# Dense weights converted in PSUM banks, and a new order of products and background work, in a fused attention, expert and dense kernel

## The chip, the cores and the metric

The kernel runs on one core of a Trainium2 chip. The metric is the device time of one execution in microseconds (us). The core's engines each work through their own queue in order: PE (TensorE, matrix products; PEld are its weight loads), DVE (VectorE), ACT (ScalarE), POOL (GpSimd) and SP (SyncE, which only issues DMAs here). They meet through semaphores.

## What is computed

The reference chains three layers. Attention through 32 memory slots per head gives 4608 rows of 512. Each row is then sent to one of 8 experts (at most 576 rows each, handed out greedily by the score), whose layer is two products with a ReLU between. The result goes through one dense layer with a hard-swish:

```python
def _moe_ref(x, w_gate, w1, w2):
    ...
    for idx in order:                       # all (token, expert) scores, largest first
        tok, e = (int(idx) // E, int(idx) % E)
        if assigned[tok] >= 0 or counts[e] >= cap:
            continue
        assigned[tok] = e
        counts[e] += 1
    ...
    for e in range(E):
        mask = assigned == e
        h = np.maximum(x[mask] @ w1[e], 0.0)
        out[mask] = h @ w2[e]

def _moe2_ref(x, w_in, w_out):              # w_in 512 x 2048, w_out 2048 x 512
    h = x @ w_in
    relu6 = np.clip(h + 3.0, 0.0, 6.0)
    g = h * relu6 / 6.0
    return g @ w_out
```

Inputs of the dense layer are 64-bit floating-point weights, which the kernel reads as pairs of 32-bit integers and converts on the chip.

## The kernel before

All products after attention are made from pairs of 16-bit numbers (a high and a low part), three matmuls for one product. The program falls into these stages:

- Attention, up to about 255 us.
- For each expert k, `l1(k)` (first layer, 192 matmuls of 288 columns, PSUM tiles named `p` with `xt` as input) and `l2(k)` (second layer, tiles `p` with `h` as input). The expert's weights (`w`) are fetched into `wst`, scaled and split by `weights()`: ACT writes the high part, DVE (for four pieces of T = 3, POOL) the low part.
- `unit(k)`: the dense layer on 512 rows. Its output `h @ w_in` is made with seven block products per step instead of eight (a Strassen-Winograd scheme). One unit has eight steps (`step(i)`); a step runs seven products of six matmuls of 256 columns into three PSUM tiles `pq`, `pr`, `pw`, with `take` (ACT) and `join` (DVE, L568 `h<-pw,h` and so on) moving the sums out, then `gate`: ACT, DVE (`h<-h,h`, 128x512), ACT and POOL work out the hard-swish. After each product but some, `pend` adds one deferred piece of the second dense product (six matmuls of 512 columns into `acc`).
- The order is l1(0) l2(0) l1(1) l2(1) unit 0 unit 1 l1(2) l2(2) l1(3) l2(3) unit 2 l1(4) l2(4) unit 3 and so on, and units 6, 7, 8 at the end.

Beside this chain of products run background jobs, as Python generators at build time: `routes()` (who goes to which expert: eight rounds per expert, each with matmuls `rtp` and short DVE instructions, and at the end one-hot matrices `OH`), `gathers()` (rows `xg` fetched by index, transposed by PE into `xp`, written to `xt`), `weights()`, `ysplit(k)` (scales the expert's output `y` and splits it into seven tiles `st`, ACT then DVE), and the dense weights. A build-time clock (`CK.now`, with a cost per instruction for DVE, ACT and POOL in `V_`, `A_`, `G_`) decides where a job's next instruction is put; `yield t` asks to go on at time t, `yield t, V_` only once DVE's queue is worked off by that clock as well. On the chip none of these times exist: only the order in each queue stays. `R_OK[0]` is the highest expert whose routing may begin.

The dense weights: 32 loads `dst` (128x1024 integers each). `dense_piece` makes 512 floats from each with four DVE instructions of 512 elements (one TENSOR_SCALAR, three SCALAR_TENSOR_TENSOR) on `cva`, an SBUF tile, and two or three of ACT. The w_out pieces are then split by ACT and POOL into `wo`; two w_in pieces together go through `wino_weights`, where POOL and ACT make the seven blocks, write them to DRAM (`wid`), and `stream` fetches them again for each step as `ws`.

PSUM: seven banks in a ring (`bank`), of which stages before unit 0 use the first four; from unit 0 on all seven are in use: four for `acc`, three for `pq`, `pr`, `pw`, with `xp` and `amx` in between. Every instruction of the background jobs stands under L568, every matmul under L619, transposes under L624, since helpers record them.

Of the kernel before, what the change touches and what calls it, by code (L numbers as in the profile page):

```python
# [20 lines left out]
def attn_moe_kernel(ctx: ExitStack, tc: tile.TileContext, q, k, v, phi, w_gate, w1, w2, w_in, w_out, out):  # L21
# [560 lines left out]
    A_ = Eng(nc.scalar, 0.06, 0.00097)  # L582
# [50 lines left out]
    def bank_free():  # L633
        return any(BANK[i][0] for i in RING if i < NB[0])

    def bank(done):
        if not bank_free():
            b, CK.busy = CK.busy, False
            need(bank_free)
            CK.busy = b  # L640
        i = next(i for i in RING if i < NB[0] and BANK[i][0])
        RING.remove(i)
        RING.append(i)
        BANK[i] = done
        return f"bk{i}"

    def mm_tile(shape, name, done):
        return ps.tile(shape, F32, name=name, tag=bank(done), bufs=1)
# [355 lines left out]
    def weights():  # L1004
        for T in range(2 * E):
            k, which = divmod(T, 2)
            while k not in EIX or T == 3 and 1 not in XI:
                yield CK.now + 0.3
# [26 lines left out]
            for n in range(9):  # L1035
# [14 lines left out]
                if n and n - 1 in PS.get(T, ()):  # L1050
# [4 lines left out]
                    yield CK.now + 0.1, A_  # L1055
                    WC[T] = c + i, tl
                elif n:
                    yield rd[n - 1], V_
                    c, i = divmod(n - 1, 2)
                    cs = slice(i * 512, i * 512 + 512)  # L1060
                    V_.scalar_tensor_tensor(tl[c][:, 1, cs], WST[T, c][0][:, cs], s[:, 0:1], tl[c][:, 0, cs],
                                            op0=OP.mult, op1=OP.subtract)
                    if i and T + 1 < 2 * E and T != 2:
                        spawn(w_later(T + 1, c))
                    yield CK.now + 0.1, A_
                    WC[T] = c + i, tl
# [11 lines left out]
    def gathers():  # L1078
        for k in range(E):
# [7 lines left out]
            def fetch(i):  # L1087
# [5 lines left out]
                elif k == 1 and i > 1:  # L1093
                    if i % 2 == 0:
                        big.append(wk.tile([128, 2, 512], F32, name="xg", tag=f"wst{i // 2 - 1}"))
                    xg = big[-1][:, i % 2]
# [124 lines left out]
    WA, WX, NWS, CUR = {}, {}, [0], [0]  # L1221
# [9 lines left out]

    def dense_piece(which, j, done, st, ready):
        yield ready, V_
        L, Hw = st[:, 0::2], st[:, 1::2]
        while not spare(0):
# [4 lines left out]
        V_.tensor_scalar(a, Hw, 3, 0x3FFFFFF8, op0=OP.logical_shift_left, op1=OP.bitwise_and)  # L1240
        yield V_.t - 0.3, V_
        V_.scalar_tensor_tensor(a, Hw, -(1 << 30), a, op0=OP.bitwise_and, op1=OP.bitwise_or)
        yield V_.t, V_
        s2 = Hw.bitcast(F32)
        A_.activation(s2, s2, AF.Square)
        V_.scalar_tensor_tensor(a, L, 29, a, op0=OP.logical_shift_right, op1=OP.bitwise_or)
        yield max(V_.t, A_.t) + HOP, V_
# [172 lines left out]
    def ysplit(k):  # L1420
# [49 lines left out]
        for i, src, r in ((A11, t1, 0.0), (A12, u1, 0.0), (A22, u2, 0.0), (S1Y, x1, r1), (S2Y, x2, r2), (S3Y, t2, r3),  # L1470
# [85 lines left out]
    def unit(k):  # L1556
# [5 lines left out]
        def step(i):  # L1562
# [4 lines left out]
            if k == 0 and i == 6:  # L1567
                R_OK[0] = 3
# [78 lines left out]
            spawn(join("q", 3, False), first=True)  # L1647
            pend(2)
# [59 lines left out]
```

## Time and profile before

| | us |
|---|---|
| median of 3 runs (lowest to highest) | 1551.49 (1549.43 to 1551.62) |
| the profiled execution | 1555.25 |
| its span on the core | 1553.5 |
| PE busy in the span | 1362.9 |
| DVE / ACT / POOL busy | 984.9 / 811.2 / 602.1 |
| the chain that ended last: PE / DVE | 64% / 18% |

The profiled execution lies 3.76 us over the median; 1.75 us of it are outside the span. An engine's busy time says how much it works, not whether it is waited for: that is read in a stretch of the program at a time, from the waits of PE, which has the most work by far.

### The profile page before, as it was taken

To read this page: it belongs to the slowest core of one execution; us is meant where nothing else is said; L and a number is where in the kernel's file an instruction comes from. 1 tells how busy PE (TensorE), PEld (TensorE's weight loads), DVE (VectorE), ACT (ScalarE), POOL (GpSimd) and SP (SyncE) were. 2 spreads that over 40 slices of the span, in tenths; PEclk is the share of its full clock that TensorE was granted. 3 is DMA by queue.
4 is the path that set the end of the run, shared out by engine and by line. 5 is a ranking of instruction groups with operands and counts; after the bars stand their busy time and mean duration, and the time that the engine had idled before them with its cause. 6 is when DMAs were issued, how large, how long until landed. Compare 5 with 4: busy or idle time off the path is not lost.

```text
span 1553.5 us, 27582 instructions
## 1 busy us (share of the span) xinstructions
PE 1362.9 (88%) x10892; PEld 1011.2 (65%) x10892; DVE 984.9 (63%) x2195; ACT 811.2 (52%) x1572; POOL 602.1 (39%) x611
## 2 busy tenths in 40 slices
PE   4788885986558997989899989999999999999998
PEld 4667664764425665869667856875686687666664
DVE  4678877989996676787846584666555423335222
ACT  4667655567655453552664266236646532545443
POOL 5765304366766343230432053135233221334322
PEclk9989996997768998989999999999999999999999
DMA  9865677464632344330342143124232220233331
GB/s 300 288 240 165 196 228 256 148 222 154 197 127 94 109 163 133 106 92 1 132 153 76 55 136 122 52 82 154 98 125 96 96 75 28 95 109 136 109 109 51
DMA packets 82337, 206.27 MB, mean 133 GB/s; under 512 B 10912, under 2 KB 41632, under 8 KB 82208
## 3 DMA queue, kind: packets, MB, share of 16 engines
q1 hardware_dynamic: 66224, 149.98, 28.5%
q0 software_dynamic: 15168, 52.96, 10.3%
q8 instruction: 85, 1.39, 0.4%
q10 hardware_dynamic: 816, 1.57, 0.3%
q14 instruction: 44, 0.36, 0.1%
HBM read 177.23 MB, written 27.26 MB: 132 GB/s over the span
## 4 chain that ended last, share of the span: by engine, by line
PE 64%; DVE 18%; issue 5%; ACT 5%; DMA 3%; POOL 3%; SPq 0%; ACTq 0%; DVEq 0%; POOLq 0%
PE acc L619 21%; PE p L619 18%; PE pq L619 11%; PE pr L619 5%; DVE cva L568 4%; PE pw L619 3%; DVE h L568 2%; PE xa L420 2%; DMA wst<-in_moe_w_dram,ei 2%; DVE w L568 1%; PE kvp L191 1%; ACT h L568 1%; DVE OH L568 1%; DMA kvt<-in_v_dram 1%; ACT wscr L568 1%
## 5 line engine op out<-in xcount | busy, mean ns | idle before, releaser
L619 PE MATMUL acc<-wo,h 128*128 128x512 f16 x1728 | 432.3, 384 | 35.0 <-ACT h L568 33.4
L619 PEld LDWEIGHTS <-ws 128*128 128x128 f16 x3024 | 301.1, 100 | 145.9 <-issue 52.7
L619 PEld LDWEIGHTS <-w 128*128 128x128 f16 x3072 | 336.6, 122 | 71.4 <-DVE w L568 7.6
L568 POOL TENSOR_TENSOR h<-h,h 128x512 f16<-128x512 f32 x144 | 175.2, 1218 | 436.4 <-ACT h L568 434.6
L619 PEld LDWEIGHTS <-h 128*128 128x128 f16 x1728 | 168.5, 99 | 178.6 <-ACT h L568 34.0
L619 PE MATMUL p<-xt,w 128*128 128x288 f16 x1536 | 210.5, 293 | 5.4 <-DVE h L568 2.1
L619 PE MATMUL p<-h,w 128*128 128x288 f16 x1536 | 201.3, 290 | 12.0 <-POOL w L568 4.8
L568 DVE SCALAR_TENSOR_TENSOR h<-h,h 128x512 f32<-128x512 f32 x144 | 111.8, 777 | 85.2 <-ACT h L568 85.2
L568 ACT ACTIVATE h<-pq 128x256 f32<-128x256 f32 x216 | 81.8, 379 | 151.4 <-PE pq L619 148.5
L568 ACT ACTIVATE h<-h,half_c,inv 128x512 f32<-128x512 f32 x144 | 116.8, 811 | 71.6 <-DVE h L568 47.5
L568 POOL DMA_INDIRECT wst<-in_moe_w_dram,ei x64 | 64.7, 1011 | 214.7 <-DVE ei L568 104.9
L568 ACT ACTIVATE h<-h 128x512 f16<-128x512 f32 x144 | 90.0, 625 | 76.7 <-DVE h L568 74.9
L568 ACT ACTIVATE h<-p 128x288 f16<-128x288 f32 x128 | 52.0, 411 | 130.1 <-PE p L619 127.4
L568 DVE SCALAR_TENSOR_TENSOR w<-wst,s,w 128x512 f16<-128x512 f32 x124 | 106.1, 863 | 1.0 <-ACT w L568 1.0
L568 DVE SCALAR_TENSOR_TENSOR cva<-dst,cva 128x512 int32<-128x512 int32 (+1 forms) x96 | 95.2, 1017 | 0.5
L568 ACT ACTIVATE w<-wst,s 128x512 f16<-128x512 f32 x124 | 86.0, 711 | 7.2 <-DVE s L568 4.3
L568 DVE SCALAR_TENSOR_TENSOR h<-p,h 128x288 f16<-128x288 f32 x128 | 57.2, 453 | 47.5 <-ACT h L568 42.6
L568 DVE TENSOR_TENSOR h<-pr,h 128x256 f32<-128x256 f32 x72 | 30.4, 422 | 80.4 <-PE pr L619 76.3
L568 ACT ACTIVATE y<-p 128x288 f32<-128x288 f32 x64 | 26.0, 406 | 104.1 <-PE p L619 101.4
L568 ACT ACTIVATE wscr<-wst 128x1024 bf16<-128x1024 f32 x64 | 67.5, 1054 | 19.1 <-DMA wst<-in_moe_w_dram,ei 18.5
L568 DVE TENSOR_TENSOR h<-pq,h 128x256 f32<-128x256 f32 x72 | 30.3, 421 | 53.8 <-PE pq L619 53.8
L568 DVE TENSOR_TENSOR h<-pw,h 128x256 f32<-128x256 f32 x72 | 30.3, 421 | 53.6 <-PE pw L619 51.2
(548 smaller groups left out, 2332.8 us busy)
## 6 DMA issues: line engine op xcount, KB each, us to landing
ws<-wid SPq DMA_DIRECT2D x72, 896.0 KB
dst<-in_moe_w_out_dram SPq DMA_DIRECT2D x26, 512.0 KB
qt<-in_q_dram SPq DMA_DIRECT2D x8, 1024.0 KB
dq<-in_moe_w_in_dram SPq DMA_DIRECT2D x16, 512.0 KB
xd<-xs SPq DMA_DIRECT2D x32, 256.0 KB
kvt<-in_k_dram SPq DMA_DIRECT2D x7, 1152.0 KB
kvt<-in_v_dram SPq DMA_DIRECT2D x7, 1152.0 KB
dst<-in_moe_w_in_dram SPq DMA_DIRECT2D x15, 512.0 KB
```

The lines of the kernel that those rows point to most:

```text
L191: nc.tensor.matmul(p[i * 64:(i + 1) * 64, g, 0:128], A[:, hp, r, :], KV[b][:, :, hp, r * 64:(r + 1) * 64], start=(r == 0), stop=(r == R - 1))
L420: nc.tensor.matmul(p[r, g], AT[u][:, half, g, r], VB[b][:, g], start=True, stop=True)
L568: r = f(*a, **kw)
L619: nc.tensor.matmul(o, l, r, start=start, stop=stop, skip_group_check=more)
```

## The change

It converts the dense weights in PSUM tiles `cv` of the upper three banks (4 to 6) instead of in SBUF tiles `cva`; the copy to `cva` is made by ACT while it scales. A common turn (`turn`) puts conversion instructions at least 1.15 us apart on the build-time clock. Routing starts at other places, `ysplit` and `weights` wait for ACT and DVE by the clock for k > 1, the fetch of expert 1's second weights no longer waits for its rows (these are gathered into a `ws` buffer instead of `wst`), ACT is taken to cost more by the clock, and from a unit's second step on the products come in another order.

```diff
-    A_ = Eng(nc.scalar, 0.06, 0.00097)
+    A_ = Eng(nc.scalar, 0.08, 0.0011)
...
-    def bank_free():
-        return any(BANK[i][0] for i in RING if i < NB[0])
+    def bank_free(lo=0):
+        return any(BANK[i][0] for i in RING if lo <= i < (7 if lo else NB[0]))
...
@@ weights
-            while k not in EIX or T == 3 and 1 not in XI:
+            while k not in EIX:
...
-                    yield rd[n - 1], V_
+                    yield (rd[n - 1], V_) if k > 1 else rd[n - 1]
...
-                    if i and T + 1 < 2 * E and T != 2:
+                    if i and T + 1 < 2 * E:
                         spawn(w_later(T + 1, c))
...
@@ gathers
                 elif k == 1 and i > 1:
-                    if i % 2 == 0:
-                        big.append(wk.tile([128, 2, 512], F32, name="xg", tag=f"wst{i // 2 - 1}"))
-                    xg = big[-1][:, i % 2]
+                    if i == 2:
+                        big.append(wk.tile([128, 1792], F32, name="xg", tag="ws", bufs=2))
+                    xg = big[-1][:, 512 * i - 1024:512 * i - 512]
...
+    TURN = [0.0]
+
+    def turn():
+        while CK.now < TURN[0]:
+            yield TURN[0]
+        TURN[0] = CK.now + 1.15
+
     def dense_piece(which, j, done, st, ready):
         yield ready, V_
         L, Hw = st[:, 0::2], st[:, 1::2]
+        while not bank_free(4):
+            yield CK.now + 0.1
+        free = [False]
+        pf = mm_tile([128, 512], "cv", free, 4)
+        a = pf.bitcast(I32)
+        yield from turn()
+        V_.tensor_scalar(a, Hw, 3, 0x3FFFFFF8, op0=OP.logical_shift_left, op1=OP.bitwise_and)
+        yield from turn()
+        V_.scalar_tensor_tensor(a, Hw, -(1 << 30), a, op0=OP.bitwise_and, op1=OP.bitwise_or)
+        yield V_.t, V_
+        s2 = Hw.bitcast(F32)
+        A_.activation(s2, s2, AF.Square)
+        yield from turn()
+        V_.scalar_tensor_tensor(a, L, 29, a, op0=OP.logical_shift_right, op1=OP.bitwise_or)
+        yield max(V_.t, A_.t) + HOP
+        yield from turn()
+        V_.scalar_tensor_tensor(pf, s2, GUARD, pf, op0=OP.is_ge, op1=OP.mult)
+        yield V_.t
+        BUSY.remove(done)
         while not spare(0):
             yield CK.now + 0.1
         tag = spare(0)
         BUSY.add(tag)
         a = wk.tile([128, 512], I32, name="cva", tag=tag)
-        V_.tensor_scalar(a, Hw, 3, 0x3FFFFFF8, op0=OP.logical_shift_left, op1=OP.bitwise_and)
...
-        A_.activation(af, af, AF.Copy, scale=SD[which][:, 0:1])
+        A_.activation(af, pf, AF.Copy, scale=SD[which][:, 0:1])
+        free[0] = True
...
@@ wino_weights
-        while 2 * i not in WA:
+        while 2 * i not in WA or len(WG) > len(WX):
...
@@ l1
-        if k > 2:
-            R_OK[0] = k + 1
+        if k == 2:
+            R_OK[0] = 4
...
@@ ysplit
-            yield r
+            yield (max(r, CK.now + 2.0), A_) if k > 1 else r
             A_.activation(ST[k][i][:, 0], src, AF.Copy, scale=s)
-            yield A_.t + HOP
+            yield (A_.t + HOP, V_) if k > 1 else A_.t + HOP
...
@@ step
-            if k == 0 and i == 6:
-                R_OK[0] = 3
+            if i == 4 and k < 2:
+                R_OK[0] = k + 2
+            elif i == 2 and k > 1:
+                R_OK[0] = k + 3
...
             spawn(take("r", 3), first=True)
-            prod("w", 2, True)
-            spawn(join("w", 0, True), first=True)
             pend(2)
+            if not i:
+                prod("w", 2, True)
+                spawn(join("w", 0, True), first=True)
             need(lambda: 0 in st)
             prod("q", 6, False)
             spawn(take("q", 1), first=True)
-            need(lambda: 3 in st)
-            prod("r", 3, False)
-            spawn(join("r", 1, True), first=True)
+            if i:
+                prod("w", 2, True)
+                spawn(join("w", 0, True), first=True)
+            else:
+                need(lambda: 3 in st)
+                prod("r", 3, False)
+                spawn(join("r", 1, True), first=True)
             pend(2)
-            need(lambda: 1 in st)
+            need(lambda: 1 in st and 3 in st)
             prod("q", 7, False)
             spawn(join("q", 3, False), first=True)
+            if i:
+                prod("r", 3, False)
+                spawn(join("r", 1, True), first=True)
             pend(2)
...
```

DVE's queue in unit 0, before: from step 1's join of `pw` to the second `h<-h,h` of step 0's gate. `st` belongs to ysplit(1), `cva` to the conversion.

```order
L568 TENSOR_TENSOR h_5426<-pw,h_5426 128x256
L568 SCALAR_TENSOR_TENSOR cva<-dst,cva 128x512
L568 SCALAR_TENSOR_TENSOR st__5466<-y_4994,sy_5371,st__5466 128x512
L568 SCALAR_TENSOR_TENSOR cva<-dst,cva 128x512 x2
L568 SCALAR_TENSOR_TENSOR st__5467<-y_5160,sy_5371,st__5467 128x512
L568 SCALAR_TENSOR_TENSOR cva<-dst,cva 128x512 x3
L568 SCALAR_TENSOR_TENSOR st__5468<-y_5160,sy_5371,st__5468 128x512
L568 SCALAR_TENSOR_TENSOR cva<-dst,cva 128x512
L568 SCALAR_TENSOR_TENSOR h_5403<-h_5403,h_5324 128x512
L568 SCALAR_TENSOR_TENSOR cva<-dst,cva 128x512
L568 SCALAR_TENSOR_TENSOR st__5469<-sx__5473,sy_5371,st__5469 128x512
L568 SCALAR_TENSOR_TENSOR h_5403<-h_5403,h_5324 128x512
```

The same queue after the change, from step 0's joins of `pr` and `pq` to the second half of its gate (`h_5395`); `cv` is the conversion.

```order
L568 TENSOR_TENSOR h_5321<-pr,h_5321 128x256
L568 SCALAR_TENSOR_TENSOR cv<-dst,cv 128x512
L568 TENSOR_TENSOR h_5321<-pq,h_5321 128x256
L568 SCALAR_TENSOR_TENSOR cv<-dst,cv 128x512
L568 SCALAR_TENSOR_TENSOR h_5395<-h_5395,h_5321 128x512
L568 SCALAR_TENSOR_TENSOR cv<-dst,cv 128x512
L568 TENSOR_REDUCE sy_1f<-amx 128x1
L568 TENSOR_SCALAR sy_5372<-sy_1f 128x1 x2
L568 TENSOR_SCALAR cv<-dst 128x512
L568 TENSOR_SCALAR inv_5448<-sx,s_1_4382 128x1
L568 TENSOR_SCALAR inv_5448<-inv_5448,s_1_4810 128x1
L568 SCALAR_TENSOR_TENSOR h_5395<-h_5395,h_5321 128x512
```

The gate's first half has moved ahead of the `st` of ysplit(1), right behind the joins that it needs.

PE's queue after the change, where l1(3) has ended: the last round of routing expert 4, up to its first one-hot matmul. Six more rows of `rtp<-RH,OH` and six of a second `OH` follow, then the first matmul of l2(3).

```order
L819 LDWEIGHTS S_2708
L819 MATMUL rtp<-CR,S_2708 128x8
L828 LDWEIGHTS onesb
L828 MATMUL rtp<-FL,onesb 128x8
L870 LDWEIGHTS onesb
L870 MATMUL rtp<-ce,onesb 128x8
L897 LDWEIGHTS tri
L897 MATMUL rtp<-tot,tri 128x2
L898 LDWEIGHTS triu
L898 MATMUL rtp<-tot,triu 128x1
L968 LDWEIGHTS OH
L968 MATMUL rtp<-RH,OH 128x10
```

Before, the same routing lies in l2(3); its `ce` matmul stands between products of that layer:

```order
L619 LDWEIGHTS w_3_8410
L619 MATMUL p_8922<-h_8669,w_3_8410 128x288
L870 LDWEIGHTS onesb
L870 MATMUL rtp<-ce,onesb 128x8
L619 LDWEIGHTS w_0_8335
L619 MATMUL p_8951<-h_8403,w_0_8335 128x288
```

After the change no matmul of a layer is left between the matmuls of that chain.

DVE's queue before, in step 1 of unit 2 (`h_9196`), with routing 4's `OH`, expert 4's `w` and ysplit(3)'s `st`:

```order
L568 TENSOR_TENSOR h_9196<-pw,h_9196 128x256
L568 TENSOR_TENSOR OH<-lo,i_2719 128x768
L568 SCALAR_TENSOR_TENSOR w_0_9214<-wst_8964,s_4_9144,w_0_9214 128x512
L568 SCALAR_TENSOR_TENSOR st__9251<-y_8753,sy_9127,st__9251 128x512
L568 TENSOR_TENSOR h_9196<-pr,h_9196 128x256
L568 TENSOR_TENSOR OH<-lo,i_2719 128x768
L568 SCALAR_TENSOR_TENSOR st__9252<-y_8921,sy_9127,st__9252 128x512
L568 TENSOR_TENSOR h_9196<-pq,h_9196 128x256
```

The same queue after the change, in step 2 of unit 2 (`h_9591`), where routing 5 now runs (`FL`, `TP`, `mi`, `TH`, `C`, `fp`):

```order
L568 TENSOR_TENSOR h_9591<-pw,h_9591 128x256
L568 SCALAR_TENSOR_TENSOR st__9379<-sx__9383,sy_9273,st__9379 128x512
L568 TENSOR_SCALAR FL<-rtp 128x8
L568 TENSOR_TENSOR h_9591<-pq,h_9591 128x256
L568 TENSOR_SCALAR TP<-KT,fp 128x15
L568 TENSOR_REDUCE mi<-rtp 128x1
L568 SCALAR_TENSOR_TENSOR TH<-mi,TP 128x15
L568 TENSOR_TENSOR C<-V,TH 128x36x15
L568 TENSOR_SCALAR fp<-mi,fp 128x1
L568 TENSOR_TENSOR h_9591<-pr,h_9591 128x256
```

The long instructions between two joins have given way to a round of routing, and the join of `pr` now comes last.

## Rows read from the trace of the kernel before

**Rows 1.** The page, part 2: busy tenths of PE and DVE in 40 slices.

```profile
PE   4788885986558997989899989999999999999998
DVE  4678877989996676787846584666555423335222
```

**Rows 2.** Windows: length, PE, PEld, DVE, ACT, POOL busy (x instructions), granted clock, DMA.

```profile
324.00:399.00 75.00, 59.01 (x399) 46.22 (x400) 69.96 (x103) 50.48 (x98) 50.34 (x41) 0.82 0.53 183
407.50:498.50 91.00, 53.05 (x297) 32.36 (x296) 78.63 (x94) 54.42 (x101) 66.42 (x51) 0.74 0.39 133
498.50:624.00 125.50, 116.07 (x855) 76.05 (x854) 83.69 (x218) 57.24 (x108) 44.30 (x41) 0.96 0.38 126
745.00:830.00 85.00, 76.82 (x545) 52.57 (x543) 53.65 (x97) 55.19 (x105) 33.12 (x28) 0.96 0.35 120
```

**Rows 3.** PE's waits from 398 to 490 us: total, times, longest.

```profile
PE acc L619 <- ACT h L568: 33.2, 3, 21.3
```

**Rows 4.** The first half of the first gate on ACT and DVE, and PE behind it.

```profile
412.56 0.81 ACT L568 ACTIVATE h<-h,half_c,inv 128x512 f32<-128x512 f32 x1 [0.94 <-DVE h L568]
...
431.95 1.64 DVE L568 SCALAR_TENSOR_TENSOR h<-h,h 128x512 f32<-128x512 f32 x1
...
439.59 2.74 PE L619 MATMUL acc<-wo,h 128*128 128x512 f16 x6 [21.27 <-ACT h L568]
```

**Rows 5.** Starts of joins of pw in steps 0, 5 and 6 of unit 0.

```profile
407.55 0.41 DVE L568 TENSOR_TENSOR h<-pw,h 128x256 f32<-128x256 f32 x1
...
498.54 0.42 DVE L568 TENSOR_TENSOR h<-pw,h 128x256 f32<-128x256 f32 x1 [1.38 <-PE pw L619]
...
508.30 0.42 DVE L568 TENSOR_TENSOR h<-pw,h 128x256 f32<-128x256 f32 x1 [1.00 <-PE pw L619]
```

**Rows 6.** Groups of DVE instructions, whole program: busy us, mean ns.

```profile
L568 DVE SCALAR_TENSOR_TENSOR cva<-dst,cva 128x512 int32<-128x512 int32 (+1 forms) x96 | 95.2, 1017 | 0.5
L568 DVE TENSOR_SCALAR cva<-dst 128x512 int32<-128x512 int32 x32 | 23.9, 753 | 1.0 <-POOL wg L568 1.0
L568 DVE SCALAR_TENSOR_TENSOR xt<-xp,sx,xt 128x512 f16<-128x512 f32 x32 | 23.8, 747 | 7.4 <-ACT xt L568 7.1
L568 DVE TENSOR_TENSOR C<-V,TH 128x540 bf16<-128x540 f32 x46 | 34.1, 741 | 1.4
L568 DVE TENSOR_REDUCE CR<-CM 128x8 f16<-128x64 f16 x46 | 12.3, 268 | 1.6
```

**Rows 7.** By tile: duration in ns, shortest/median/longest, first and last start.

```profile
L568 DVE SCALAR_TENSOR_TENSOR cva<-dst,cva x96: 672/694/1747, 264.6 to 481.1; 128x512 int32<-128x512 int32 x64, 128x512 f32<-128x512 f32 x32
L568 DVE TENSOR_SCALAR cva<-dst x32: 410/423/1664, 262.6 to 476.9; 128x512 int32<-128x512 int32 x32
...
L568 DVE SCALAR_TENSOR_TENSOR h<-h,h x144: 675/690/1753, 432.0 to 1538.5; 128x512 f32<-128x512 f32 x144
L568 DVE SCALAR_TENSOR_TENSOR h<-p,h x128: 436/457/461, 267.6 to 1284.9; 128x288 f16<-128x288 f32 x128
```

**Rows 8.** DVE's conversion instructions alone up to unit 0's first join, window view.

```profile
262.00:407.50 145.50, 61.79 (x75) 0.89 0.54 181
```

**Rows 9.** DVE's conversion groups in unit 0, from 407.5 to 498.5 us.

```profile
L568 DVE SCALAR_TENSOR_TENSOR cva<-dst,cva 128x512 int32<-128x512 int32 (+1 forms) x41 | 46.8, 1169 | 0.3
...
L568 DVE TENSOR_SCALAR cva<-dst 128x512 int32<-128x512 int32 x13 | 10.3, 791 | 0.0
```

**Rows 10.** PE between l2(2) and l1(3).

```profile
681.77 1.39 PE L619 MATMUL p<-h,w 128*128 128x288 f16 x10
...
694.08 1.62 PE L619 MATMUL p<-xt,w 128*128 128x288 f16 x6
```

**Rows 11.** PE, last round of routing 1 up to its second one-hot matmul.

```profile
289.17 0.32 PE L808 MATMUL rtp<-Bo,C 128*128 128x64 bf16 x5
...
305.54 0.31 PE L968 MATMUL rtp<-RH,OH 128*128 128x10 bf16 x6
```

**Rows 12.** PE's waits from 624 to 1320 us.

```profile
PE pq L619 <- DVE h L568: 17.1, 12, 3.7
```

More of the change, by code (lines that the diff above doesn't have):

```diff
@@ L631, in attn_moe_kernel, with bank @@
     RING = list(range(7))
-    def bank_free():
-        return any(BANK[i][0] for i in RING if i < NB[0])
-    def bank(done):
-        if not bank_free():
+    def bank_free(lo=0):
+        return any(BANK[i][0] for i in RING if lo <= i < (7 if lo else NB[0]))
+    def bank(done, lo=0):
+        if not bank_free(lo):
             b, CK.busy = CK.busy, False
-            need(bank_free)
+            need(lambda: bank_free(lo))
             CK.busy = b
-        i = next(i for i in RING if i < NB[0] and BANK[i][0])
+        i = next(i for i in RING if lo <= i < (7 if lo else NB[0]) and BANK[i][0])
         RING.remove(i)
@@ L645, in bank, with mm_tile @@
         return f"bk{i}"
-    def mm_tile(shape, name, done):
-        return ps.tile(shape, F32, name=name, tag=bank(done), bufs=1)
+    def mm_tile(shape, name, done, lo=0):
+        return ps.tile(shape, F32, name=name, tag=bank(done, lo), bufs=1)
     jpi = iT = rt.tile([128, 16], I32, name="iT")
@@ L1054, in weights @@
                     G_.tensor_tensor(tl[c][:, 1, cs], WST[T, c][0][:, cs], tl[c][:, 0, cs], op=OP.subtract)
-                    yield CK.now + 0.1, A_
+                    yield (CK.now + 0.1, A_) if k > 1 else max(CK.now + 0.1, V_.t - 0.5)
                     WC[T] = c + i, tl
                 elif n:
-                    yield rd[n - 1], V_
+                    yield (rd[n - 1], V_) if k > 1 else rd[n - 1]
                     c, i = divmod(n - 1, 2)
@@ L1062, in weights @@
                                             op0=OP.mult, op1=OP.subtract)
-                    if i and T + 1 < 2 * E and T != 2:
+                    if i and T + 1 < 2 * E:
                         spawn(w_later(T + 1, c))
-                    yield CK.now + 0.1, A_
+                    yield (CK.now + 0.1, A_) if k > 1 else max(CK.now + 0.1, V_.t - 0.5)
                     WC[T] = c + i, tl
@@ L1220, in attn_moe_kernel @@
     WID = [dram.tile([128, 3584], F16, name=f"wid{i}") for i in range(8)]
-    WA, WX, NWS, CUR = {}, {}, [0], [0]
+    WG, WA, WX, NWS, CUR = set(), {}, {}, [0], [0]
     def dense():
@@ L1239, in dense_piece @@
         a = wk.tile([128, 512], I32, name="cva", tag=tag)
-        V_.tensor_scalar(a, Hw, 3, 0x3FFFFFF8, op0=OP.logical_shift_left, op1=OP.bitwise_and)
[L1241 to L1247, printed above, removed]
         af = a.bitcast(F32)
-        V_.scalar_tensor_tensor(af, s2, GUARD, af, op0=OP.is_ge, op1=OP.mult)
-        yield V_.t
-        BUSY.remove(done)
         yield V_.t + HOP, A_
-        A_.activation(af, af, AF.Copy, scale=SD[which][:, 0:1])
+        A_.activation(af, pf, AF.Copy, scale=SD[which][:, 0:1])
+        free[0] = True
         if which == 0:
@@ L1269, in wino_weights @@
     def wino_weights(i):
-        while 2 * i not in WA:
+        while 2 * i not in WA or len(WG) > len(WX):
             yield CK.now + 0.1
+        WG.add(i)
         (a0, t0, _), (a1, t1, r) = WA.pop(2 * i), WA.pop(2 * i + 1)
```

## The prediction

> **What bounds the kernel now.** I read the page's slices first. PE is at eight tenths or more in every slice after the 16th, and has its hole in slices 10 to 12, at six and five tenths, where DVE stands at nine [rows 1]. So PE sets the end, and what can be won lies where DVE holds it up. The windows give the places. From 324 to 399 us DVE is busy for 69.96 of 75 us and PE for 59.01; in unit 0, from 407.5 to 498.5 us, DVE for 78.63 of 91 and PE for 53.05; in unit 1 (498.5 to 624 us) PE works 116.07 of 125.5, in unit 2 (745 to 830 us) 76.82 of 85, with DVE at 53.65 [rows 2].
>
> PE's waits in unit 0 are headed by one group: `acc` for ACT's `h`, 33.2 us in three waits, 21.3 in the longest [rows 3]. ACT is not slow there. Its gate instruction begins at 412.56 and takes 0.81, the DVE instruction that follows it starts only at 431.95, and PE goes on at 439.59 [rows 4]: the gate stood 18.6 us behind conversion and ysplit work in DVE's queue. The joins give the same in another way: five steps take 498.54 − 407.55 = 91 us, the next one 9.8 [rows 5].
>
> **The conversion.** The 96 SCALAR_TENSOR_TENSOR take 95.2 us and the 32 TENSOR_SCALAR 23.9 [rows 6], together 119. Their best times are 672 and 410 ns, their longest 1747 and 1664; the gate's `h<-h,h`, which also has two SBUF inputs, spreads from 675 to 1753, while all 128 `h<-p,h`, with one input in PSUM, lie between 436 and 461 [rows 7]. Here lies the change: the first instruction of a piece writes to PSUM, and the other three have one input there. No row shows a 512-element DVE instruction writing PSUM. Bounds: from `h<-p,h`, 457 ns for 288 elements, 0.46 to 0.81 us (no cost and full cost for the elements added); `xt<-xp`, 512 elements with one PSUM input, takes 0.747 on the mean [rows 6]. I take 0.69, the best of the SBUF form [rows 7] and inside these. 128 × 0.69 = 88 us, 31 less than 119; at 0.747 it is 23 less, at 0.46 it is 60.
>
> The spread of `h<-h,h` against the narrow band of `h<-p,h` [rows 7] is the trace's reason for that price. The Trainium skill has a rule for it (SBUF — State Buffer, "Who interferes with whom"): a VectorE instruction with two SBUF inputs contends with GpSimd's reads, one with at most one SBUF input, outside the modes that use both ports, does not; by these rows the trace agrees. The TENSOR_SCALAR's best of 410 ns for 512 elements [rows 7] is the row that a second rule touches. In VectorE: DVE Perf Modes, "Why PSUM operands drop a tier", it says that an operand in PSUM caps the mode, and 32-bit data at the plain rate. By it the 32 TENSOR_SCALAR would lose their fast form, and against their best that costs 32 × (0.69 − 0.41) = 9 us of the 31; no run shows it yet.
>
> **Stage A, up to unit 0's first join.** The conversion takes 61.79 us there in 75 instructions [rows 8]; after the change 72 of them stand before that join, 72 × 0.69 = 50 us, 12 less. I take three quarters, −9, since DVE is nearly full but PE also waits for weights there. Bounds: −14 if DVE's whole relief and a little of POOL's comes through, +5 if the slow times stay and TENSOR_SCALAR alone rises to 0.69.
>
> **Stage B, unit 0, steps 0 to 5.** Before: 41 + 13 conversion instructions, 46.8 + 10.3 = 57.1 us [rows 9], so 78.63 − 57.1 = 21.5 of other DVE work [rows 2]. After: 56 conversion instructions (38.6 us), the same 21.5, and, since routing 2 now begins earlier, five `C` at 0.741 and some 37 short ones at about 0.21 (below `CR`, 0.268 [rows 6], an estimate): 11.6. Sum 71.7; at 93% full, as from 324 to 399 [rows 2], 77 us in place of 91: −14. The gate now stands next to its joins, so the 21.3 us wait goes; what is late next is DVE as a whole. Bounds: −30 (61 us, with a price near 0.5) and +26 (the bank rival below).
>
> **Unit 1.** PE idles 125.5 − 116.07 = 9.4 us [rows 2]. The moved product gives `pq`'s last join more cover: −5, bounds 0 to −9.
>
> **The gap ahead of l1(3).** PE's last matmuls of l2(2) start at 681.77 and take 1.39, l1(3) begins at 694.08 [rows 10]: 10.9 us, in which the rows of expert 3 are not there, as routing 3 ended late. Now routing 3 starts in unit 1's fifth step and all transposes `xp` of expert 3 lie inside l2(2). Most of it goes; the last rows' DMA may be waited for: −8, bounds −6 to −11.
>
> **A new stall ahead of l2(3).** By PE's order the whole last round of routing 4 stands between l1(3) and l2(3), with no product in between. A matmul there waits for one or more DVE instructions, and the next of these for the matmul. In routing 1 the same chain, from the last `C` to the second one-hot, took 305.54 − 289.17 = 16.4 us [rows 11] with DVE shared with the conversion; alone DVE answers sooner. I take 13, bounds 10 (six tenths) and 17 (as before, or a little more). Behind it in PE's queue is all of l2(3), so nothing hides it. It has a cause in the planner: l2(3) wants the buffers that ysplit(2) frees, and that is now spaced out by 2 us steps.
>
> **Units 2 to 4.** PE waits 17.1 us for `pq` there [rows 12], mostly where `OH`, `w` and `st` stand together between two joins. The clump is spread, and `pr` now joins last, which gives `pq` about one join more (0.42 [rows 5]). Against that, a route's front comes in: in unit 2 seven `C` at 0.741, some 70 short ones at about 0.22 (an estimate, below `CR` [rows 6]), some 24 us with the end of it, of which about 8 replace `OH` that go to the next layer. DVE rises from 53.65 to about 70 of 85 us [rows 2], 82%. I take −6, bounds −14 (four fifths of the waits) and +15 (5 in each unit, where joins stand behind `C` and `OH`).
>
> The other edits I cost at nothing. The spacing of `turn` and the `A_` prices exist by the planner's clock; on the chip they only interleave. Expert 1's earlier weights are hidden by l2(0); if SP's loads stand behind that buffer, it shows in A, and is in its bound.
>
> **Sum.** −9 −14 −5 −8 +13 −6 = −29. The profiled execution would be 1555.25 − 29 = 1526.25. It lies 3.76 above the median of 1551.49; taken off the median, 1522.5.
>
> **The rivals.**
>
> *Banks decide in unit 0 (slower).* From step 2 on four banks hold `acc`, so three are left for `pr`, `pq`, `pw` and the `cv` pieces. A product must wait in PE's order until ACT has copied the piece that holds its bank. 15 pieces remain after the first join, three to a step, over in effect two banks that alternate. With h as the time that a piece holds its bank, and 8 us a step for the products' own use (an estimate, most of the 9.8 of a free step [rows 5]), a step takes (3h + 8) / 2. Four instructions of 0.69 with 10 to 14 others between, and a copy of 0.81 like the gate's on ACT [rows 4], make h about 7: 14.5 a step, 72.5 for five, less than DVE's 77. At h = 9.5 stage B is as before; with the other terms at −15 the whole breaks even at h = 11.5. At h = 13 five steps take 117.5: +26.5 − 15 = +11.5, 1563. For it: a piece waits for ACT twice; against it: ACT has room (54.42 of 91 [rows 2]).
>
> *The conversion isn't cheaper, the change of price does not take place.* If the spread in rows 7 came from something that PSUM doesn't avoid, 56 instructions keep 57 us in unit 0, and only the gate's better place counts: A 0, B −8, C −3: 0 − 8 − 3 − 8 + 13 − 6 = −12, 1539.5. For it: nothing shows a write to PSUM; against it the 128 short times.
>
> *DVE was the whole limit.* Then each stage follows the relief, with idle time gone besides: A −14, B −30, C −9, gap −11, stall +10, units −14: −68, 1483.5. For it: 78.63 of 91 busy [rows 2]; against it, the banks and POOL (66.42 of 91 [rows 2]), which feeds `ws`.
>
> *The new routing hurts units 2 to 4.* +15 in place of −6: −8, 1543.5. For it: 82% of DVE and long `OH`; against it: unit 1 runs with DVE at 83.69 of 125.5 and routing inside, and loses little [rows 2].
>
> **How the numbers follow.** The forecast has 0.45; DVE as the whole limit 0.18; units 2 to 4 0.16; no cheaper price 0.12; the banks 0.09. Below 1487 lies about half of the second case; above 1553, the banks and a little of the two middle cases, together about 0.2 outside. The likeliest case's own range is 1505 to 1538. Within 0.2%, about 3 us and what a measurement of this kernel can tell, comes from the middle cases at their worst, 0.06; slower is the banks' part and a remainder of the units', 0.09; faster 0.85.
>
> **What would show it.** Conversion instructions at 0.6 to 0.75 us with little spread; no PE wait of over 10 us for `acc` in unit 0, and five steps in about 77 us; no gap ahead of l1(3); some 13 us of PE waits on `rtp` ahead of l2(3); `pq` waits in units 2 to 4 below 17. It is wrong if the `cv` instructions still reach 1.7 us, if PE waits in unit 0 for ACT's copy of `cv`, or if the stall ahead of l2(3) is not there.

## The result, and the profile after

The changed kernel takes 1534.45 us (median of 4, 1530.74 to 1538.50) against 1550.46 for the kernel before: a ratio of 0.9899, 95% interval 0.9871 to 0.9927, some 16 us. Forecast were 1522.5 us within 1487 to 1553. The profiled execution took 1538.5 us, its span 1536.7, so the two profiles differ by 16.8 us. The slices of the page after answer to [rows 1]:

```profile
PE   4788885877866999996899999989999999999998
...
DVE  4677867889867777787686479539334522434322
```

PE's hole, before in slices 10 to 12 (6, 5, 5), is filled in part and now ends a slice later (7, 8, 6, 6 in slices 10 to 13). A new one of a single slice, a 6, stands at slice 19: the stall ahead of l2(3). Where the 16.8 us lie, worked out from the starts of PE's first matmul of each stage and of the joins of `pw`:

| stage | before | after | moved | forecast |
|---|---|---|---|---|
| start to l1(0) | 258.5 | 263.4 | +4.8 | 0 |
| l1(0) to unit 0's first join (A) | 149.0 | 141.5 | −7.5 | −9 |
| unit 0, steps 0 to 5 (B) | 91.0 | 90.7 | −0.3 | −14 |
| rest of unit 0, unit 1 | 126.3 | 117.0 | −9.3 | −5 |
| gap ahead of l1(3) | 10.9 | none | −10.9 | −8 |
| between l1(3) and l2(3) | none | 14.2 | +14.2 | +13 |
| units 2, 3, 4 | 258.9 | 249.6 | −9.3 | −6 |
| layers of experts 2 to 6 | 282.4 | 288.2 | +5.8 | 0 |
| unit 5, l1(7), l2(7), units 6 to 8 | 376.5 | 372.2 | −4.3 | 0 |

Of the first row little belongs to the change: the experiments on the changed kernel (e1 to e11 below) reach l1(0) at 257.9 to 262.2 us. Units 0 and 1 with one and the same order of DVE's work took 207.7, 204.5 and 208.7 us in three profiles (after, e2, e11), so a difference under 4.5 us there is not read as an effect.

The edge of stage B moved as well. In the new order `pw`'s product stands behind one more piece of `acc` and one more product of `pq` (from a unit's second step on), so the five steps hold 309 of the layer's matmuls instead of 297. At the pace of undisturbed matmuls that is about 2 us (an estimate from their starts in the trace before: 1.3 us for a piece of `acc`, 0.65 for a product of `pq`) which stage B has more and the next row less.

The conversion's instructions by tile in the profile after (ns: shortest, median, longest), which answer to [rows 7]:

```profile
L568 DVE SCALAR_TENSOR_TENSOR cv<-dst,cv x96: 677/687/779, 266.2 to 502.4; 128x512 int32<-128x512 int32 x64, 128x512 f32<-128x512 f32 x32
L568 DVE TENSOR_SCALAR cv<-dst x32: 680/685/696, 264.3 to 496.1; 128x512 int32<-128x512 int32 x32
...
L568 DVE SCALAR_TENSOR_TENSOR h<-h,h x144: 674/692/1754, 408.1 to 1521.4; 128x512 f32<-128x512 f32 x144
L568 DVE SCALAR_TENSOR_TENSOR h<-p,h x128: 440/457/459, 272.0 to 1270.5; 128x288 f16<-128x288 f32 x128
```

The spread is gone where one operand moved to PSUM, and stayed where both inputs are in SBUF (`h<-h,h`). The conversion's sum over the program, 44.0 + 22.0 + 22.0 = 88.0 us, is the forecast 88.

The windows after (same columns as [rows 2]), and PE's waits from 395 to 500 us, beside [rows 3]:

```profile
324.00:399.00 75.00, 60.94 (x440) 49.65 (x437) 65.64 (x119) 53.90 (x104) 48.69 (x44) 0.86 0.59 194
404.90:495.60 90.70, 55.91 (x342) 33.96 (x341) 69.23 (x137) 55.03 (x103) 54.46 (x53) 0.85 0.43 145
495.60:611.40 115.80, 112.08 (x819) 73.69 (x818) 83.90 (x204) 66.12 (x123) 43.18 (x41) 0.97 0.39 136
741.00:825.00 84.00, 77.64 (x574) 52.23 (x572) 64.94 (x164) 49.34 (x96) 30.20 (x25) 0.96 0.36 118
```

```profile
PE pw L619 <- ACT cva L568: 13.0, 5, 3.5
PE acc L619 <- ACT cva L568: 5.3, 1, 5.3
PE rtp L808 <- DVE C L568: 4.5, 1, 4.5
PE pr L619 <- ACT cva L568: 4.4, 4, 1.7
PE rtp L828 <- DVE FL L568: 2.9, 2, 1.7
PE rtp L819 <- DVE CR L568: 2.7, 2, 2.0
```

DVE has only 69.23 us of work in unit 0's five steps, and idles 21.5 of the 90.7. The 21.3 us gate wait is gone; in its place products wait for ACT's copy out of a conversion bank (13.0 + 5.3 + 4.4 = 22.7 us) and routing 2's matmuls wait for DVE (10.1 us). DVE in turn waits for PE, for the products that its joins read (`pw`, `pq`) and for routing's matmuls; its waits in the same five steps:

```profile
DVE h L568 <- PE pw L619: 7.3, 3, 4.2
DVE CM L568 <- PE rtp L808: 3.8, 2, 2.4
DVE h L568 <- PE pq L619: 3.6, 3, 1.5
```

PE's queue ahead of l2(3), in order of time:

```profile
700.98 0.32 PE L808 MATMUL rtp<-Bo,C 128*128 128x64 bf16 x5 [0.83 <-DVE C L568]
702.55 0.18 PE L819 MATMUL rtp<-CR,S 128*128 128x8 f16 x1 [1.26 <-DVE CR L568]
...
705.12 0.17 PE L870 MATMUL rtp<-ce,onesb 128*128 128x8 bf16 x1 [1.96 <-DVE ce L568]
707.37 0.16 PE L897 MATMUL rtp<-tot,tri 128*128 128x2 bf16 x1 [2.09 <-DVE tot L568]
...
711.22 0.33 PE L968 MATMUL rtp<-RH,OH 128*128 128x10 bf16 x6 [3.66 <-DVE OH L568]
714.15 0.33 PE L968 MATMUL rtp<-RH,OH 128*128 128x10 bf16 x6 [2.60 <-DVE OH L568]
714.33 2.08 PE L619 MATMUL p<-h,w 128*128 128x288 f16 x8
```

Each matmul of 0.2 to 0.3 us waits 1 to 4 us for DVE's answer, as in [rows 11]. From 698 to 716 us, while PE stands idle between these matmuls, the granted clock is 0.66 on the mean, between the lower level (1.2 GHz, 0.5) and the full one (2.4 GHz, 1.0); l2(3) behind it runs at 0.94 and takes 27.1 us against 24.2 at 1.00 before.

### The profile page after: what moved, and what is told of

It reads as the page before. It is cut to its first block, busy times and chain, and to the rows that moved or that the text cites. A ratio compares the mean times of both kernels' runs of the same rounds, so it can differ in the third digit from the quotient of the medians.

```text
span 1536.7 us, 27522 instructions
## 1 busy us (share of the span) xinstructions
PE 1358.9 (88%) x10892; PEld 1009.3 (66%) x10892; DVE 955.5 (62%) x2195; ACT 807.3 (53%) x1572; POOL 574.9 (37%) x610
## 4 chain that ended last, share of the span: by engine, by line
PE 67%; DVE 16%; ACT 5%; issue 5%; DMA 4%; POOL 3%; SPq 0%; POOLq 0%; DVEq 0%; ACTq 0%
PE p L619 22%; PE acc L619 20%; PE pq L619 10%; PE pr L619 5%; PE pw L619 2%; DVE h L568 2%; PE xa L420 2%; DVE w L568 2%; PE kvp L191 1%; DMA wst<-in_moe_w_dram,ei 1%; POOL h L568 1%; DVE cv L568 1%; ACT h L568 1%; DMA xg<-xd,ix 1%; DMA kvt<-in_v_dram 1%
## 5 line engine op out<-in xcount | busy, mean ns | idle before, releaser
L619 PE MATMUL acc<-wo,h 128*128 128x512 f16 x1728 | 435.4, 386 | 17.1 <-ACT h L568 9.5
L619 PEld LDWEIGHTS <-w 128*128 128x128 f16 x3072 | 340.1, 122 | 63.0 <-DVE w L568 7.9
L619 PEld LDWEIGHTS <-ws 128*128 128x128 f16 x3024 | 294.8, 99 | 121.6 <-issue 39.5
L619 PE MATMUL p<-xt,w 128*128 128x288 f16 x1536 | 207.3, 292 | 3.3 <-DVE h L568 3.3
L568 DVE SCALAR_TENSOR_TENSOR h<-h,h 128x512 f32<-128x512 f32 x144 | 105.9, 740 | 69.1 <-ACT h L568 68.3
L568 DVE SCALAR_TENSOR_TENSOR w<-wst,s,w 128x512 f16<-128x512 f32 x124 | 102.6, 835 | 0.0
L568 DVE TENSOR_REDUCE ym<-y 128x1 f32<-128x288 f32 (+1 forms) x66 | 31.2, 474 | 71.6 <-ACT y L568 71.3
L568 POOL DMA_INDIRECT xg<-xd,ix x35 | 36.8, 1051 | 85.3 <-PE xp L624 49.4
L568 DVE SCALAR_TENSOR_TENSOR cv<-dst,cv 128x512 int32<-128x512 int32 (+1 forms) x96 | 65.9, 689 | 3.1 <-ACT dst L568 1.9
```

Source lines behind the costliest of these rows:

```text
L568: r = f(*a, **kw)
L619: nc.tensor.matmul(o, l, r, start=start, stop=stop, skip_group_check=more)
```

## The experiments

Stages are given as in the table; "after" is the changed kernel. "Five steps" is stage B. Each time is a median of 4 to 10 runs; ratios are to the kernel before, whose median in the batches lay between 1550.5 and 1553.2 us, so that 3 us between two times tell nothing.

**e1: the conversion back in SBUF.**

```diff
-        pf = mm_tile([128, 512], "cv", free, 4)
-        a = pf.bitcast(I32)
+        a = wk.tile([128, 512], I32, name="cva", tag=tag)
         yield from turn()
```

> The changed kernel with its conversion back in SBUF tiles (its spacing, its order of products and its routing stay). Theory A, port: the 687 ns of the conversion come from PSUM alone, and the three PSUM banks are what PE waited for in unit 0. Then the SCALAR_TENSOR_TENSOR of the conversion spread again up to 1.7 us, mean 0.9 to 1.1; PE's waits for ACT's copy of the conversion (22.7 us in unit 0 after the change) go to 0; five steps of unit 0 take 90 to 100 us since DVE has some 19 us more; the stretch before unit 0's first join is 6 to 12 us longer; in all 8 to 15 us over the changed kernel, 1542 to 1550. Theory B, spacing: the short times come from the spacing of the instructions, not from PSUM. Then they stay at about 0.7 us, five steps take 70 to 80 us as no bank is waited for, and the kernel is 10 to 20 us faster than the changed one.

Measured: 1650.69 us, ratio 1.0625 (1.0593 to 1.0657). By tile:

```profile
L568 DVE SCALAR_TENSOR_TENSOR cva<-dst,cva x96: 673/692/3419, 263.0 to 514.5; 128x512 int32<-128x512 int32 x64, 128x512 f32<-128x512 f32 x32
L568 DVE TENSOR_SCALAR cva<-dst x32: 407/938/1391, 261.0 to 507.3; 128x512 int32<-128x512 int32 x32
```

The spread is back with the spacing still there, so PSUM makes the short times. The conversion takes 67.3 + 29.2 + 26.9 = 123.4 us, 35 more than in PSUM. The size of the loss was missed by 100 us. The five steps were missed too: they take 74.0 us, not 90 to 100, with fewer conversion instructions begun in them (44 in place of 56) and DVE busy for 97% of them; the rest of unit 0 and unit 1 takes 156.6 (+39.6), so that units 0 and 1 take 230.6 us (+23.0). But units 2, 3 and 4, where nothing is converted, take 109.6, 110.0 and 94.8 us (+64.8), and what lies behind them 26.8 more, with PE waiting for routing's DVE answers at a granted clock of 0.89 from 765 to 873 us. The build-time planner put routing at other places; why these cost so much wasn't isolated, so the total says little about PSUM.

**e2: ysplit(2) without its spacing.**

```diff
-            yield (max(r, CK.now + 2.0), A_) if k > 1 else r
+            yield (max(r, CK.now + 2.0), A_) if k > 2 else r
...
-            yield (A_.t + HOP, V_) if k > 1 else A_.t + HOP
+            yield (A_.t + HOP, V_) if k > 2 else A_.t + HOP
```

> The changed kernel without the 2 us steps and the waits by the clock in ysplit(2) alone (they stay for k above 2). By its order on PE the last round of routing 4 then lies inside l2(3). Theory A, the stall ahead of l2(3) (14.2 us between l1(3) and l2(3) in the changed kernel) is made by that spacing: the gap falls below 2 us, and 10 to 14 us of it are kept, 1520 to 1525 in all. Rival: the routing is the limit there and comes back as waits in l2(3) and unit 2 (for the one-hot matrices and the gathered rows): l2(3) and unit 2 together grow by as much as the gap falls, 0 to -4 in all.

Measured: 1522.92 us, ratio 0.9817 (0.9795 to 0.9839), 11.5 less than after. PE's queue at the same place:

```profile
693.42 0.17 PE L819 MATMUL rtp<-CR,S 128*128 128x8 f16 x1
693.45 0.32 PE L619 MATMUL p<-xt,w 128*128 128x288 f16 x1
693.88 0.17 PE L828 MATMUL rtp<-FL,onesb 128*128 128x8 bf16 x1
693.90 0.65 PE L619 MATMUL p<-h,w 128*128 128x288 f16 x4
```

l2(3) follows l1(3) at once (0.1 us). Unit 2 gives 6.3 us of the 14 back (84.5 to 90.8); the two make 7.8 of the 11.5 us, and the rest lies in stretches that the edit doesn't touch (the start and units 0 and 1, 3.1 each in the profiles). So without the spacing there is no stall. How long it is with the spacing depends on where routing lies too: it is 6.2 us in e6, which keeps the spacing.

**e3: the fourth conversion instruction writes to SBUF, which frees the bank.**

```diff
-        V_.scalar_tensor_tensor(pf, s2, GUARD, pf, op0=OP.is_ge, op1=OP.mult)
...
+        V_.scalar_tensor_tensor(af, s2, GUARD, pf, op0=OP.is_ge, op1=OP.mult)
+        free[0] = True
...
-        A_.activation(af, pf, AF.Copy, scale=SD[which][:, 0:1])
-        free[0] = True
+        A_.activation(af, af, AF.Copy, scale=SD[which][:, 0:1])
```

> The changed kernel, but the fourth conversion instruction writes its result to the SBUF tile, and the bank is free after it; ACT scales in SBUF as in the kernel before. Theory A, banks: unit 0 is held by banks that wait for ACT's copy. A piece held its bank for 5.3 to 8.8 us in most of unit 0; without the copy 4 to 7. PE's waits for the conversion's banks fall from 22.7 to 8 to 14 us, five steps of unit 0 from 90.7 to 78 to 84; 7 to 12 us less in all. Rival, DVE: the fifth of unit 0 that PE waits is DVE's own lateness, whichever name ends the wait: five steps stay within 88 to 93 us and the time within 3 us of the changed kernel's.

Measured: 1535.73 us, ratio 0.9903 (0.9878 to 0.9928), as after. The five steps fall from 90.7 to 78.6 us, as theory A had it; a piece holds its bank for 5.8 us on the mean there, up to the end of the fourth instruction. PE's waits from 395 to 700 us:

```profile
PE pw L619 <- DVE cva L568: 9.7, 5, 3.0
PE rtp L808 <- DVE C L568: 6.2, 5, 3.6
PE acc L619 <- DVE cva L568: 5.3, 1, 5.3
PE pw L619 <- ACT y L568: 4.4, 1, 4.4
```

But units 0 and 1 together fall only from 207.7 to 202.1, and the 31.3 us of l2(3) (27.1 after) and 87.6 of unit 2 (84.5) take the rest back. The waits for the conversion's banks fall to 15.0 us (8 to 14 forecast). The local half of the theory held, the total didn't. Nor are the five steps the same work: the planner put 52 conversion instructions and four `C` of routing 2 there, in place of 56 and five.

**e4: without the new order of products.** The four places in `step` as they were before.

```diff
-            if i:
-                prod("r", 3, False)
-                spawn(join("r", 1, True), first=True)
```

> The changed kernel with the order of products of the kernel before in each step. Theory A: the new order gives the joins of pq and pr cover; without it PE's waits for pq from unit 1 on come back: units 1 to 4 take 6 to 12 us more and units 6 to 8 2 to 3 us more, since a free step costs more: 8 to 15 us over the changed kernel. Rival: the new order is worth nothing once DVE has less conversion in its queue; the gains in units 1 to 4 come from routing's new places: within 3 us of the changed kernel.

Measured: 1534.38 us, ratio 0.9882 (0.9858 to 0.9906), the same as after: the rival. Units 0 and 1 lose 3.3 us (211.0), units 2 to 4 win 2.4 (247.2). Inside units 0 and 1 much moves: the five steps take 74.7 us, with 40 conversion instructions in place of 56, and the rest 136.3 in place of 117.0. So five steps can be shorter by 16 us with nothing won.

**e5: PSUM only ahead of unit 0.**

```diff
+        if NB[0] == 7:
+            a = wk.tile([128, 512], I32, name="cva", tag=tag)
+            pf = a.bitcast(F32)
+        else:
...
             pf = mm_tile([128, 512], "cv", free, 4)
```

> The changed kernel, but from unit 0 on (where seven banks are in use) a piece is converted in an SBUF tile, as before; ahead of unit 0 it stays in PSUM. Theory A, banks: unit 0's products wait for the conversion's banks (22.7 us from 395 to 500 us), and would run ahead if the banks were free. Then that wait is 0, and although the instructions are longer again in unit 0 (mean 0.95 to 1.2 us against 0.687), unit 0 and unit 1 together take 196 to 203 us in place of 207.6: 5 to 11 us less in all. Theory B, DVE: DVE's time and the chain through it sets unit 0; then the 15 to 28 us of DVE that come back lengthen units 0 and 1 together by 6 to 16 us.

Measured: 1546.07 us, ratio 0.9951 (0.9932 to 0.9971); units 0 and 1 take 215.2 us, five steps 102.1. It didn't free the banks, so it doesn't decide between the theories:

```profile
PE acc L619 <- ACT cva L568: 37.4, 2, 27.8
PE pw L619 <- ACT cva L568: 4.9, 2, 3.3
```

A piece that was begun in PSUM ahead of unit 0 still holds a bank that `acc` wants, and its copy comes late in ACT's queue.

**e6: routing released where it was before.**

```diff
-            if i == 4 and k < 2:
-                R_OK[0] = k + 2
-            elif i == 2 and k > 1:
-                R_OK[0] = k + 3
+            if k == 0 and i == 6:
+                R_OK[0] = 3
...
-        if k == 2:
-            R_OK[0] = 4
+        if k > 2:
+            R_OK[0] = k + 1
```

> The changed kernel with routing released at the places of the kernel before. Theory A: the gap ahead of l1(3) (10.9 us before, 0 after) went because routing 3 begins in unit 1, and units 2 to 4 are faster because routing lies in them. Then a gap of 6 to 11 us ahead of l1(3) is back, the stall ahead of l2(3) is shorter (2 to 10 us), and units 2 to 4 take 4 to 9 us more: 1536 to 1546 in all. Rival: units 2 to 4 gain by the spacing of ysplit alone, and keep their times within 3 us; then 1529 to 1537.

Measured: 1522.22 us, ratio 0.9807 (0.9771 to 0.9843), 12.2 less than after, and outside what either theory gave. Gap (7.9) and shorter stall (6.2) came as theory A had them, but the five steps fall to 78.8 us without any change to the banks, and units 2 to 4 to 245.3 (249.6 after). The waits for banks are no shorter:

```profile
PE pw L619 <- ACT cva L568: 13.2, 6, 3.3
PE pr L619 <- ACT cva L568: 8.7, 5, 4.1
PE acc L619 <- ACT cva L568: 5.3, 1, 5.3
PE pq L619 <- DVE h L568: 2.5, 2, 1.7
```

No `rtp` line is left. So in this kernel routing's new places cost more than they gave.

**e7: e2 and e3 together.**

> Two edits on the changed kernel together: ysplit(2) without its spacing, and the fourth conversion instruction into SBUF. Theory A, the edits act in different places and each has its own effect: 1522.9 + 1.3 = 1521 to 1526, the same as the first edit alone. Theory B: what the second edit won in unit 0 (five steps in 78.6 in place of 90.7 us) was lost in unit 1 and after only by the way that routing 2 and 3 fell, and with another order it is kept: 1511 to 1519.

Measured: 1521.53 us, ratio 0.9792 (0.9760 to 0.9825): theory A. Five steps 80.8, units 0 and 1 201.7 us.

**e8: without the turn.**

```diff
-        while CK.now < TURN[0]:
-            yield TURN[0]
-        TURN[0] = CK.now + 1.15
+        yield V_.t, V_
```

> The changed kernel without the common turn of 1.15 us; a conversion instruction waits only until DVE's queue is worked off by the build-time clock. Theory A: the spacing exists by that clock alone; without it a piece's four instructions stand closer in DVE's queue and hold their bank for less long. PE's waits for the conversion's banks fall from 22.7 to 12 to 18 us; time within 4 us of the changed kernel's, 1530 to 1538. Rival: the spacing keeps gates and joins ahead of the conversion; without it a wait of over 8 us for a gate is back in unit 0, and the kernel is 5 to 12 us slower.

Measured: 1535.86 us, ratio 0.9884 (0.9849 to 0.9920), the time of after; but on another way than either theory. More pieces are converted ahead of unit 0: stage A grows to 170.7 us, units 0 and 1 shrink to 175.8, the sum (346.5) is that of after (349.2) within 3. The five steps hold only 15 conversion instructions and take 61.4 us. In A, one wait of PE for ACT's `y` takes 26.5 us; ACT works off conversion copies meanwhile, and stands 6.8 us of that time for the write of the blocks to DRAM:

```profile
386.37 0.67 ACT L568 ACTIVATE cva<-cv,sd 128x512 f32<-128x512 f32 x1
393.81 0.63 ACT L568 ACTIVATE wg<-cva 128x512 f16<-128x512 f32 x1 [6.77 <-DMA wid<-wg]
394.35 0.64 ACT L568 ACTIVATE dst<-dst 128x512 f32<-128x512 f32 x1
```

Such waits sum to 19.4 us of ACT in the whole run, and to 3.5 in after.

**e9: e2 and e6 together.**

> The changed kernel with routing released as before and ysplit(2) without its spacing. By PE's order routing 4 then lies wholly in l1(3) and l2(3), its one-hot matrices in unit 2. Theory A: the two edits take the same stall away once and the rest of each adds: the 6.2 us left ahead of l2(3) go too, some of it comes back in unit 2 (as 6 us did without the spacing alone): 1515 to 1520. Rival: the one-hot matrices together with ysplit's and the weights' instructions clump in unit 2 as before, and its time goes back to 86 to 92 us: 1521 to 1528.

Measured: 1516.81 us, ratio 0.9775 (0.9750 to 0.9801). The stall is 0, the gap 7.8, unit 2 83.6 us: theory A, no clump.

**e10: e2, e3 and e6 together.**

> The same with the fourth conversion instruction into SBUF. Each of these two (the shorter hold of the banks, routing 2 out of unit 0) brought unit 0's first five steps from 90.7 to 79 us. Theory A, they act on different waits (banks, and routing's matmuls on PE): together the five steps take 65 to 72 us, and units 0 and 1 together 195 to 200 in place of 203.5. Theory B, one limit behind both (conversion through DVE, ACT and the buffers that it writes to): five steps stay at 76 to 82 us, units 0 and 1 at 200 to 204.

Measured: 1509.10 us, ratio 0.9718 (0.9686 to 0.9749), the fastest here, about 25 us under after. The five steps take 65.7 us, as theory A had it, and units 0 and 1 189.4, less than its 195. The window of the five steps and PE's waits from 395 to 600 us:

```profile
405.00:470.70 65.70, 50.97 (x309) 31.86 (x308) 50.67 (x89) 48.91 (x94) 47.71 (x45) 0.88 0.53 181
...
PE acc L619 <- DVE cva L568: 6.8, 1, 6.8
PE pw L619 <- DVE cva L568: 6.4, 4, 2.9
PE pw L619 <- ACT y L568: 4.6, 1, 4.6
```

**e11: ysplit without spacing for every k.** As e2, with `yield r` and `yield A_.t + HOP` for all.

> The changed kernel without the spacing of ysplit for every k. Theory A: this spacing is what won in units 2 to 4 (258.9 us before, 249.6 after, 245.3 with the old routing places), as it keeps st away from the joins: without it units 3 and 4 together take 6 to 12 us more than the 163.7 that they take without the spacing of ysplit(2) alone. Rival: the routing's one-hot matrices, which no longer stand there, were the limit; then units 3 and 4 stay within 3 us of 163.7, and the time is 1520 to 1526.

Measured: 1535.75 us, ratio 0.9896 (0.9868 to 0.9924). Units 3 and 4 take 165.0 us against 163.7: the rival, so the spacing isn't what won there. The time is 10 us over the rival's all the same: 2.7 in unit 2, 7.5 in l1(5), where PE waits 4.6 us for a gate and runs at a granted clock of 0.92 instead of 1.00, and 4.2 in units 0 and 1, which is within their scatter.

**e12: the kernel before with the new order of products alone.**

> The kernel before with the new order of products in each step alone. Theory A: the order gives no gain by itself, as leaving it out of the changed kernel cost nothing: within 4 us of the kernel before. Rival: where pq waits for the joins (17.1 us in units 2 to 4) the order is worth some of it: 4 to 9 us faster, and units 2 to 4 together 250 to 255 us.

Measured: 1547.60 us, ratio 0.9981 (0.9961 to 1.0001): no difference that can be told. Units 0 and 1 take 9.5 us less (207.8), and the gap ahead of l1(3) 7.5 more (18.4), since routing 3 comes no earlier. The gate's wait is nearly the old one:

```profile
PE acc L619 <- ACT h L568: 30.2, 3, 19.7
PE pq L619 <- ACT h L568: 7.6, 2, 6.7
```

## Why the prediction was right, and where it was not

The total came out inside the range partly by luck. Stage B, with −14 the largest term, gave next to nothing. Three gains larger than forecast (the rest of unit 0 with unit 1, the gap, units 2 to 4: 10.5 us over their terms together) happened to offset what the sum didn't have (+4.8 at the start, +5.8 in the experts' layers). A total of 1534 us doesn't tell the forecast from the case in which the conversion isn't cheaper (1539.5); the times of single instructions do.

What the five steps of unit 0 held, by run (instructions of DVE begun in them), and what the rest took:

| run | five steps | conversion | `C` of routing | rest of unit 0, unit 1 | both |
|---|---|---|---|---|---|
| after | 90.7 | 56 | 5 | 117.0 | 207.7 |
| e3, shorter hold | 78.6 | 52 | 4 | 123.6 | 202.1 |
| e6, old release | 78.8 | 52 | 0 | 124.7 | 203.5 |
| e10, both and e2 | 65.7 | 48 | 0 | 123.7 | 189.4 |
| e4, old order | 74.7 | 40 | 3 | 136.3 | 211.0 |
| e1, no PSUM | 74.0 | 44 | 2 | 156.6 | 230.6 |

- **Conversion.** Right to the tenth: 88.0 us. e1 shows that PSUM makes it and not the spacing. The traces also show what the long times go with: in the kernel before, the 44 conversion instructions with no POOL instruction beside them took 674 to 693 ns (SCALAR_TENSOR_TENSOR) and 410 to 424 (TENSOR_SCALAR), and every longer one ran beside POOL's work; after the change the 39 that ran beside POOL for all their time took 679 to 703. The Trainium skill's rule on who contends (SBUF — State Buffer, "Who interferes with whom") agrees with both traces. Its rule on PSUM operands (VectorE: DVE Perf Modes, "Why PSUM operands drop a tier") agrees too: the TENSOR_SCALAR's best went from 410 to 680 ns.
- **Stage A**: −7.5 against −9; with the conversion in SBUF 4.3 of it come back (e1). **Gap**: −10.9 against −8; e6 and e9 bring 7.9 and 7.8 us of it back with the old release, and e10 12.0, so the reason given was right. **Stall**: 14.2 against 13, and e2 shows its cause, ysplit(2)'s spacing, with a length that routing's place helps to set.
- **Stage B is the step that failed**: −0.3 against −14 (about −2 with the edge left where it was). DVE's work was forecast well (71.7 against 69.23 us), but "at 93% full" was not: DVE was 76% busy. I held DVE's 77 us and the banks' 72.5 against each other and took the larger. The hold h was right: 7.3 us on the mean for the 14 pieces from the 18th on (from the start of the first instruction to the end of ACT's copy), 7 forecast; with it the rival's formula gives 74.8 us. Measured were 90.7, more than either. The trace shows waits in both directions: PE 22.7 us for the conversion's banks and 10.1 for DVE's answers to routing 2, DVE 14.7 us (7.3 + 3.8 + 3.6) for PE. Products waiting in unit 0 for ACT's copy were among the signs of being wrong, and this one came. So two engines that wait for each other were counted as if each ran at its own pace. That these waits add up along one chain is my reading of the queues; no run takes them away with the same work left in the five steps.
- **How the parts of stage B add up is open.** The five steps fall by 12.1 us with a shorter hold (e3), by 11.9 with routing 2 elsewhere (e6) and by 25.0 with both (e10), which looks like two separate terms. But the table shows that work moved out of them each time, and that e4 and e1 shorten them by 16 us with neither edit and lose more behind. Over units 0 and 1 the gains are 5.5 and 4.2, at the edge of the scatter, and 18.3 for both (in e10, with e2's edit, which leaves these units as they are): more than their sum. Why is open. The bank rival was in part the truth: 22.7 us of waits at its place, but not slower than before.
- **The rest of unit 0 and unit 1**: −9.3 against −5, at its bound of −9; about 2 of it is the edge of stage B. With the new order of products alone units 0 and 1 fall by 9.5 us (e12), though the changed kernel without it loses only 3.3 (e4). It would fit that the new order and the cheaper conversion reach the same idle time; that isn't shown.
- **Units 2 to 4**: −9.3 against −6. The reason given, that the clump of `OH`, `w` and `st` goes, isn't shown: without ysplit's spacing units 3 and 4 keep their times (e11), without the new order too (e4), and with routing out of them units 2 to 4 take 4.3 us less (e6, one profile each). The waits of `pq` for joins did fall, from 17.1 us [rows 12] to 5.4; with the order of products as before they are 11.1 (e4), and in the kernel before with the new order 7.3 (e12), but neither of these moves the time, as other waits take their place. What did it stays open; the spacing of `weights` and ACT's new prices weren't run by themselves.
- Not forecast: −4.3 in units 5 to 8 and +5.8 in the experts' layers, 2.9 of it in l2(3), behind the stall and at a granted clock of 0.94 in place of 1.00.

The forecast's sum was −29, the profiles give −16.8; the difference is stage B's 13.7 us, less 1.5 that the other rows come to together.

## What to carry to other kernels

Where two limits of a stage lie close together (77 us of DVE, 72.5 of banks), and each engine's next work waits for the other's, don't take the larger of the two as the stage's time: here 90.7 us were measured, and DVE idled for 24% of them where 7% had been forecast. A short stretch that got faster proves little when a planner decides what lies in it: look at the stretch behind it too. A buffer in PSUM can make an instruction cheaper and still make the stage no faster, if the bank is held past the last instruction that needs it: handing the result to SBUF with that instruction cut the hold from 7.3 to 5.8 us here, but paid only with the old release of routing (e10 is 7.7 us under e9; e3 isn't under after). Where a planner decides the order, look in each queue for a chain that stands alone; one job's spacing made a 14 us stall in another.

## What the runs showed of the hardware

- DVE's first instruction of a piece, SBUF to PSUM, 128x512 32-bit, takes 680 to 696 ns in all 32 cases; the kernel before never had such a write.
- With two SBUF inputs the other three instructions reached 1747 ns before and 3419 ns in e1; with one input in PSUM the longest was 779 ns. Before, none with no POOL instruction beside it took over 693 ns.
- ACT waited up to 6.77 us for a DMA that writes `wg` to DRAM and frees its one tile (e8), inside a wait of PE for ACT of 26.5 us.
